# Start and end of an attention and MLP kernel rearranged: two float32 tiles, four DMA transposes, statistics on ScalarE, low halves on GpSimd, and a bank of its own for the last half tile

## The chip, the cores and the metric

The kernel runs on one core of a Trainium2 chip. The metric is the time of one execution on the device in microseconds (us). The engines are TensorE (PE in the profile, with PEld for its weight loads), VectorE (DVE), ScalarE (ACT), GpSimd (POOL) and SyncE (SP), which issues every DMA of this kernel from one queue, in order. Each engine, too, works through its own list in order: an instruction that waits holds up all that stands behind it on that engine.

## The reference

The input x is a sequence of 2048 tokens with 512 channels. It is normalised, and two branches read the result xn; the output is x + s * silu(m).

```python
xn = _layernorm(x)
# A: 32 heads of 16 channels; each token attends to 8 tokens, 2 apart, itself the first
qkv = (xn @ wqkv).reshape(B, S, 3, H, Dh)
logits = q . k at pos - 2*w (w = 0..7), scale Dh**-0.5, masked where pos - 2*w < 0
s = (softmax(logits) applied to v).reshape(B, S, D) @ wo
# B: normalise again, 512 -> 1376 -> 512
y = _layernorm(xn)
h = _gelu(y @ w1 + b1)
m = h @ w2 + b2
return x + s * _silu(m)
```

All arrays are float32.

## The kernel before, in words

**Tiling.** The dilation of 2 splits the tokens into an even and an odd class (c = 0, 1) of 1024 tokens each, and a class into 8 tiles of 128 tokens (i = 0..7). The 32 heads form 4 blocks of 8 heads (hb). A unit u is one class and one block; there are 8 units, class 0 first. For a unit `qkv` (L673) multiplies each of the 8 tiles with a block of 128x384 weights (q, k and v), and ScalarE scales the sums out of PSUM into one of two buffers `U`, alternating. DMAs then shift keys and values by one partition (the halos, L718), and `attention` (L737) works on VectorE with help from GpSimd. `mlp1` and `mlp2` (L948, L983) do the MLP in 4 chunks of 512 tokens and 11 blocks of 128 hidden channels, and are spread between the units as filler for TensorE. `wo_first` and `wo_last` multiply the attention with wo, class 0 in the middle of the program and class 1 at its end.

**Float16 pairs.** TensorE multiplies in float16 with a high and a low half for each operand: three products, hi·hi, lo·hi and hi·lo, so that a tile of `qkv` takes 12 matmuls of 384 columns and a step of the MLP 12 of 512. A high half is a scaled copy (ScalarE, L448, L499, L644); the low half is the source minus the high half (VectorE, L449, L501, L645). The scale is a power of two from the sum of squares of the whole weight, which ScalarE adds up (L394, L477) and TensorE totals over the partitions (L403, L408).

**The start.** `LOADS` (L48) fixes the order of the first loads: `("t", i)` is tile i already transposed, `("q", k)` half of the first or second block of wqkv, `("x", i)` tile i. Behind them come w1 in four pieces, w2, b1 and the rest of w2. Tiles 5, 6 and 7 (`FP`) get their first `qkv` in float32, straight from the transposed input: the mean is taken off (`center`, L557) and `direct` (L575) multiplies, 4 matmuls of 384 columns for a tile, with no transposition and no halves needed. The others go through `ln0` (statistics, L586), `y0` (normalise on the engine that `Y_ENG` names, transpose on TensorE, L641, then the two halves) and 12 matmuls each. Tiles 5 to 7 go through `y0` later for the second unit and the MLP. 24 matmuls without use (L1102, `WAKE`) fill gaps early on.

**Class 1.** `ln1` (L647) normalises the odd tokens: eight loads and statistics on VectorE (L542, L543), factors for all tiles with two powers on GpSimd (L529, L536), then tile by tile a second load, the normalisation and the halves, and a DMA transposition into `yT` (L666). The load of tile i waits until tile i-2 has been transposed.

**What sets the order.** Every operation is entered in a plan with an engine, an assumed duration, what it reads and writes and a priority. `issue` (L212) then orders each engine by assumed times and priorities. A number such as `PW2` or `PEV` moves whole groups of operations on their engines.

**The end.** `wo_last` (L898) first does 9 of 12 matmuls for each of the 8 tiles of class 1, those of the first three blocks, and the last 3 when the last block is there; VectorE multiplies with the gate (L939), VectorE or GpSimd adds x (L867, L869) and SP sends the tile out. The last tile is finished in two halves of 256 columns (L926, L930, L933), both in one PSUM bank.

Of the kernel before, what the change touches and what calls it, by code (L numbers as in the profile page):

```python
# [31 lines left out]
NFB = 7  # L32

W1C = [0, 2048, 4096, 5120, KT * F]
W1P = [(0, 1), (1, 2), (2, 4), (4, 6), (6, 8), (8, 10), (10, 11)]
W1FIRST = 2
# [4 lines left out]
FP = (5, 6, 7)  # L41
XC = FP
BYDMA = ()
TRZ = (0, 3, 0, 3, 0, 1, 2, 3)
PTR = 0.08
# [11 lines left out]
W2LATE = 4  # L57
# [214 lines left out]
PW2, PS2 = 0.9, 0.74  # L272
PWQ1, PW1 = 0.5, 0.75
PEV = 0.15

PTOT = 0.5

WAKE = 24
PS1 = 0.72
# [12 lines left out]
WINDOW = 0.05  # L292
PURG, WURG = 0.14, 0.05
# [6 lines left out]
def tile_mixer(ctx, tc, a_x, a_xt, a_wqkv, a_wo, b_w1, b_b1, b_w2, out):  # L300
# [171 lines left out]
    def scale_q(hb):  # L472
        col = R_s.new()
        for k in range(0, KT, 2):
            def go(k=k):
# [5 lines left out]
                aps=2, holds=stkey[hb])  # L481
# [7 lines left out]
    def prep_q(hb):  # L489
# [3 lines left out]
        for k in range(0, KT, st):  # L493
# [7 lines left out]
            dve(n, lambda src=src, dst=dst: nc.vector.scalar_tensor_tensor(  # L501
                dst[1], src(), qsc[:, hb, 0:1], dst[0], op0=ALU.mult, op1=ALU.subtract),
                r + hk, [("wq", hb, j) for j in range(k, k + st)], holds=stkey[hb], c=0.125,
                prio=PQLO if hb == 0 else None)

# [5 lines left out]
    def factors(n, mv, mk, cdst, ckeys, bias=True, close=None, pp=None, **k):  # L511
# [19 lines left out]
        with pl.fuse():
            dve(n, lambda: nc.vector.tensor_scalar(a0(), V(), EPS, None, op0=ALU.add), mk, [(A, 0)], c=0.15)
            dve(n, lambda: nc.vector.reciprocal(a1(), a0()), [(A, 0)], [(A, 1)], c=0.2)
            dve(n, lambda: nc.vector.tensor_tensor(a1(), a1(), V(), op=ALU.mult), [(A, 1)] + mk, [(A, 1)], c=0.2)
            dve(n, lambda: nc.vector.tensor_scalar(a1(), a1(), EPS, None, op0=ALU.add), [(A, 1)], [(A, 1)], c=0.2)
        pool(0.42 + 0.14 * n, lambda: nc.gpsimd.tensor_tensor(  # L536
            cdst, a1(), halves[:, 8:8 + n], op=ALU.pow), [(A, 1)], ckeys, port=False)
        return rb, p0b
# [18 lines left out]
    def center(i):  # L557
# [11 lines left out]
        pe(1, P, lambda: nc.tensor.matmul(b.t[:, 0:P], mean1, f3()[:, 0], start=True, stop=True), [f], [b], fp32=6, prio=0.04)  # L569
# [42 lines left out]
    def y0(i):  # L612
# [5 lines left out]
        if Y_ENG[i] == "act":  # L618
            with pl.fuse("act"):
# [4 lines left out]
                    [xkey, ("rb", g), ("rm", i)], [xkey, yk], aps=2)  # L624
        else:
            dve(512, lambda: nc.vector.tensor_scalar(x(), x(), mv0[:, q, 0:1], rb0[:, q:q + 1], op0=ALU.subtract,
                                                     op1=ALU.mult), [xkey, ("rb", g), ("mv0", i)], [xkey, yk], f=0.72, c=0.11)
        if i in BYDMA:
# [6 lines left out]
                [y16, (y16, 0)], [("yh", 0, i), ("y", 0, i)], rate=150e3, issue=2.1, tail=1.4)  # L635
# [6 lines left out]
        pe(4, P, tr, [yk, xkey], [b], fp32=2.4, prio=PTR + pl.prio * 1e-3)  # L642
        p3 = lambda: b.t.rearrange("p (k t) -> p k t", k=KT)
        act(512, lambda: nc.scalar.copy(hi, p3()), [b], [("yh", 0, i)], aps=0)  # L644
        dve(512, lambda: nc.vector.tensor_tensor(lo, p3(), hi, op=ALU.subtract), [b, ("yh", 0, i)], [("y", 0, i)], port=False)  # L645

    def ln1():  # L647


        mv1 = sb.tile([P, NI, 2], F32, name="mv1")  # L650
        mk = [("mv1", i) for i in range(NI)]
# [4 lines left out]
        rb = factors(NI, lambda: mv1, mk, cT[:, 1, :], [("c", 1, i) for i in range(NI)])  # L656
        for i in range(NI):
# [4 lines left out]
            y_act(lambda x=x: x.t, rb, i, [], lambda x=x: x.t, x)  # L662
# [8 lines left out]
    IORD, IORD0, IORD1 = [1, 2, 3, 4, 5, 6, 7, 0], [5, 6, 7, 0, 1, 2, 3, 4], [0, 1, 2, 3, 4, 5, 6, 7]  # L671

    def qkv(c, hb, u):  # L673
# [10 lines left out]
                [("c", c, i) for i in g] + ([("rb", gof[i]) for i in g] if g[0] in FP else [("qi", hb)]), [(cs, g)], prio=0.15)  # L684
# [4 lines left out]
        for n, i in enumerate((IORD0, IORD1)[u] if u < 2 else IORD):  # L689
# [14 lines left out]
            for n0, n1 in zip([0] + ends, ends):  # L704
# [3 lines left out]
            act(384, lambda i=i, b=b: nc.scalar.activation(  # L708
                U3[:, i:i + 31:15, :], b.t[:, 0:384].rearrange("p (t e) -> p t e", t=3),
# [356 lines left out]
    for n in range(4):  # L1066
        load_w1(n)
# [231 lines left out]
```

## Time and profile before

| | |
|---|---|
| three executions | 419.18, 419.77 and 420.14 us, median 419.77 |
| the profiled execution | 420.04 us, its span 418.3 us |
| granted TensorE clock | 1.000 |
| TensorE busy | 408.4 us (98%) |
| VectorE busy | 386.3 us (92%) |
| ScalarE busy | 213.6 us (51%) |
| GpSimd busy | 110.7 us (26%) |

The profile has a page for the whole execution and views that can be asked for a stretch of time. In a row of the timeline stand the start and the duration in us, the engine, the line, the operation, what is written from what, the shape and the count; in brackets, the idle time before it and what ended that. A float32 matmul leaves two records. The span is 1.7 us shorter than the execution that it belongs to.

### The profile page before, as it was taken

The numbers are of one execution on the slowest core, as the hardware profiler recorded it, in microseconds if no ns is written. First come the engines' busy times: TensorE is split into PE (matmuls) and PEld (weight loads), VectorE is DVE, ScalarE is ACT, GpSimd is POOL, SyncE is SP. The second block draws the span as 40 slices with busy tenths as digits, with TensorE's granted clock in tenths as the row PEclk, the third lists the DMA queues.
The fourth block names the chain that finished last, engine by engine and source line by source line (L and its number), as shares of the span: only waits on it lengthen the run. The fifth ranks groups of instructions, "written<-read, shape, count | busy, mean of one in ns | idle before, by whom it ended". The sixth has DMA issues, their size and how long they took to land.

```text
span 418.3 us, 5534 instructions
## 1 busy us (share of the span) xinstructions
PE 408.4 (98%) x2082; PEld 207.4 (50%) x2082; DVE 386.3 (92%) x395; ACT 213.6 (51%) x322; POOL 110.7 (26%) x124
## 2 busy tenths in 40 slices
PE   8899999999999999999999999999999999999995
PEld 5466544444654455445544554455445544444442
DVE  5977899999999999899999899999999998999974
ACT  3899993952539335764475336133322285236400
POOL 3310200004340555021523160425042504250022
PEclk9999999999999999999999999999999999999999
DMA  7955360220047203746275007021623465008142
GB/s 270 415 214 147 98 209 2 86 91 0 1 114 187 67 1 84 155 101 98 55 139 202 0 21 193 2 76 29 208 78 102 110 143 163 0 2 235 33 134 100
DMA packets 43130, 45.62 MB, mean 109 GB/s; under 512 B 27576, under 2 KB 28016, under 8 KB 42592
## 3 DMA queue, kind: packets, MB, share of 16 engines
q1 hardware_dynamic: 43104, 45.28, 37.6%
q8 instruction: 16, 0.26, 0.3%
q14 instruction: 10, 0.08, 0.1%
HBM read 24.32 MB, written 7.34 MB: 76 GB/s over the span
## 4 chain that ended last, share of the span: by engine, by line
PE 68%; DVE 15%; issue 7%; ACT 5%; DMA 3%; SPq 1%; POOL 0%; DVEq 0%; ACTq 0%
PE z L992 19%; PE ps L698 19%; PE ps L956 18%; PE ps L876 7%; DVE prod L810 3%; PE z L876 2%; DVE prod L752 2%; DVE w L449 2%; DVE h L978 2%; DMA prod<-in_A_x_dram 2%; PE pl L698 1%; DVE f L664 1%; DVE L L755 1%; DMA U<-U 1%; DVE prod L805 1%
## 5 line engine op out<-in xcount | busy, mean ns | idle before, releaser
L956 PE MATMUL ps<-yT,w 128*128 128x512 f16 (+1 forms) x528 | 120.8, 379 | 0.5 <-DVE h L978 0.5
L698 PE MATMUL ps<-wq,yT 128*128 128x384 f16 x696 | 115.9, 326 | 1.4 <-ACT yT L644 0.8
L992 PE MATMUL z<-w,h 128*128 128x512 f16 x480 | 110.3, 379 | 0.2 <-ACT f L1008 0.2
L698 PEld LDWEIGHTS <-yT 128*128 128x128 f16 x732 | 71.1, 98 | 50.6 <-issue 1.2
L956 PEld LDWEIGHTS <-w 128*128 128x128 f16 (+1 forms) x528 | 52.9, 100 | 61.5 <-issue 0.8
L973 ACT ACTIVATE ps<-ps,b1T,hsc 128x512 f32<-128x512 f32 (+1 forms) x44 | 32.8, 748 | 86.3 <-PE ps L956 86.2
L752 DVE TENSOR_TENSOR prod<-U 128x2048 f32<-128x2048 f32 x32 | 74.3, 2326 | 2.1 <-DMA U<-U 1.0
L992 PEld LDWEIGHTS <-h 128*128 128x128 f16 x480 | 46.7, 98 | 55.7 <-issue 0.5
L755 DVE TENSOR_REDUCE L<-prod 128x128 f32<-128x2048 f32 x32 | 72.9, 2280 | 0.4
L810 DVE TENSOR_TENSOR prod<-pl,U 128x2048 f32<-128x2048 f32 x28 | 63.2, 2281 | 1.8 <-POOL prod L820 1.8
L708 ACT ACTIVATE U<-ps,cs 128x384 f32<-128x384 f32 x58 | 33.6, 581 | 58.1 <-PE ps L698 57.9
L820 POOL TENSOR_TENSOR prod<-prod,prod 128x2048 f32<-128x2048 f32 x7 | 31.7, 4526 | 115.1 <-DVE prod L810 115.1
L830 POOL TENSOR_TENSOR prod<-prod 128x1024 f32<-128x1024 f32 x14 | 32.8, 2345 | 0.0
L978 DVE SCALAR_TENSOR_TENSOR h<-ps,hsc,h 128x512 f16<-128x512 f32 x40 | 29.3, 740 | 2.7 <-ACT h L976 2.6
L876 PE MATMUL ps<-wo,oT 128*128 128x512 f16 x132 | 29.8, 379 | 0.0
L876 PEld LDWEIGHTS <-oT 128*128 128x128 f16 x189 | 18.5, 98 | 22.1
L829 POOL COPY gate<-prod 1x1 f32<-1x1 f32 x21 | 4.4, 211 | 88.4 <-DVE prod L752 88.4
L976 ACT ACTIVATE h<-ps,hsc 128x512 f16<-128x512 f32 x40 | 26.9, 685 | 0.8
L805 DVE TENSOR_TENSOR prod<-prod,prod 128x2048 f32<-128x2048 f32 x9 | 20.5, 2280 | 0.0
L973 ACT ACT_TABLE_LOAD x10 | 12.8, 1283 | 9.2 <-PE ps L956 9.1
L830 POOL TENSOR_TENSOR prod<-prod,prod 128x1024 f32<-128x1024 f32 x7 | 16.4, 2347 | 0.0
L793 ACT ACTIVATE o<-prod,osc 128x1024 f16<-128x1024 f32 (+1 forms) x9 | 9.5, 1053 | 12.2 <-POOL prod L830 6.8
(165 smaller groups left out, 356.4 us busy)
## 6 DMA issues: line engine op xcount, KB each, us to landing
f<-in_A_x_dram SPq DMA_DIRECT2D x31, 256.0 KB, 3.4
U<-U SPq DMA_DIRECT2D x16, 392.0 KB, 4.0
gd<-f SPq DMA_DIRECT2D x12, 256.0 KB, 2.9
prod<-in_A_x_dram SPq DMA_DIRECT2D x8, 256.0 KB, 6.3
oT<-in_B_w_dram SPq DMA_DIRECT2D x2, 1024.0 KB
yT<-in_B_w_dram SPq DMA_DIRECT2D x2, 1024.0 KB, 12.1
f<-gd SPq DMA_DIRECT2D x8, 256.0 KB, 2.9
out_dram<-f SPq DMA_DIRECT2D x8, 256.0 KB
```

The costliest lines, as they stand in the source:

```text
L698: nc.tensor.matmul(b.t[:, 0:384], y[:, s, k, o:o + P], wq[:, hb, t, k], start=(n == 0), stop=(n == 11))
L708: act(384, lambda i=i, b=b: nc.scalar.activation(U3[:, i:i + 31:15, :], b.t[:, 0:384].rearrange("p (t e) -> p t e", t=3), AF.Identity, sca ...
L752: dve(2048, lambda p2=p2, g=g: nc.vector.tensor_tensor(p2(), q, slots(Ut, KH, 2 * g), op=ALU.mult), qk + [("kh", ub, 0), ("kh", ub, 1), (" ...
L755: dve(2048, lambda pr=pr, g=g: nc.vector.tensor_reduce(L3()[:, 2 * g:2 * g + 2], pr.t.rearrange("p (r f d) -> p r f d", r=2, d=DH), AX.X, ...
L810: dve(2048, lambda: nc.vector.tensor_tensor(pr.t.rearrange("p (r f d) -> p r f d", r=2, d=DH), A3()[:, 2 * g:2 * g + 2].rearrange("p r (f ...
L820: pool(4.75, lambda: nc.gpsimd.tensor_tensor(acc.t, acc.t, p1.t, op=ALU.add), [acc, p1], [acc])
L830: nc.gpsimd.tensor_tensor(x.t[:, 0:1024], x.t[:, 0:1024], y(), op=ALU.add)
L876: nc.tensor.matmul(b.t, oT[:, hb, i // 4, s, i % 4], wo[:, t, hb], start=(hb == 0 and n == 0), stop=(hb == last and n == 2))
L956: nc.tensor.matmul(b.t[0:M], w1[:, s, f * 512 + k * M:f * 512 + (k + 1) * M], yT[ch][:, t, k], start=(n == 0), stop=(n == 11))
L973: act(512, lambda: nc.scalar.activation(b.t[0:M], b.t[0:M], AF.Gelu_apprx_tanh, bias=b1T[0:M, f:f + 1], scale=hsc[0:M, 1:2]), [b, ("b1T",) ...
L978: dve(512, lambda: nc.vector.scalar_tensor_tensor(lo()[0:M], b.t[0:M], hsc[0:M, 2:3], hi()[0:M], op0=ALU.mult, op1=ALU.subtract), [b, hk], ...
L992: nc.tensor.matmul(z.t, hl[s][0:K, t * P:(t + 1) * P], w2[0:K, w, f], start=(f == 0 and n == 0), stop=(f == NF - 1 and n == 2))
```

## The change

It alters the start of the program, `ln1` and `wo_last`, and many of the plan's numbers.

- **Float32 tiles.** Only tiles 6 and 7 are multiplied in float32. Tile 7 gets its mean from four matmuls (`MEANBY`), no longer from GpSimd. Tile 5 goes the way of the others for its first `qkv`.
- **DMA transposes.** Tiles 4 to 7 (`BYDMA`) are no longer transposed on TensorE: their halves are made in SBUF, and a DMA transposes them. These DMAs wait until all of w1 has landed, and the loads of w2 wait for them. Tiles 0 to 3 keep the transposition on TensorE.
- **Order of loads.** `LOADS` covers w1, w2 and b1 as well, and tile 2 is loaded ahead of tile 0.
- **Engines.** Tables name the engine of each small step: the normalisation of tiles 0 and 5 and four low halves (two of the first block of wqkv, one of w1, one of w2) go to GpSimd, as two instructions each; the results of 4 tiles of the first unit and 3 of the second leave PSUM on VectorE.
- **Statistics of class 1.** ScalarE takes them: a pass for the sum, a small one for minus the mean, a pass for the squares.
- **The end.** The second half of the last tile gets a bank of its own and does all its 12 matmuls after the first half is done.

```diff
-W1FIRST = 2
+W1FIRST = 3
-FP = (5, 6, 7)
-XC = FP
-BYDMA = ()
-TRZ = (0, 3, 0, 3, 0, 1, 2, 3)
-GROUPS = [(0,), (1,), (2, 3, 4), (5, 6, 7)]
-BATCHES = [(0, 1, 2, 3, 4), (5, 6, 7)]
-LOADS = [("t", 5), ("t", 6), ("q", 0), ("q", 2), ("x", 0), ("x", 1), ("t", 7), ("q", 4), ("q", 6), ("x", 2), ("x", 3),
-         ("x", 4), ("x", 5), ("x", 6), ("x", 7)]
+FP = (6, 7)
+XC = (6, 7)
+BYDMA = (4, 5, 6, 7)
+TRZ = (3, 3, 0, 2, 0, 1, 1, 0)
+GROUPS = ((0,), (1, 2), (3, 4, 5), (6, 7))
+BATCHES = ((0, 1, 2, 3, 4, 5), (6, 7))
+LOADS = (('t', 6), ('q', 0), ('q', 2), ('x', 2), ('x', 0), ('q', 4), ('t', 7), ('x', 5), ('x', 1), ('x', 3), ('x', 4), ('q', 6), ('w', 0), ('w', 2), ('x', 7), ('c', 2), ('s', 1), ('c', 0), ('w', 3), ('x', 6), ('w', 1), ('c', 1), ('b', 0), ('s', 0))
+HI_ENG = ('act', 'act', 'act', 'dve', 'dve', 'dve', 'dve', 'act')
-Y_ENG = {0: "act", 1: "dve", 2: "act", 3: "act", 4: "act", 5: "dve", 6: "dve", 7: "dve"}
-W1ENG = ["dve", "dve", "act", "act", "act", "act", "act"]
+Y_ENG = ('pool', 'act', 'dve', 'dve', 'act', 'pool', 'dve', 'act')
+W1ENG = ('act', 'dve', 'act', 'act', 'act', 'act', 'act')
-W2LATE = 4
+W2LO = ('dve', 'dve', 'dve', 'dve', 'dve', 'pool', 'dve')
+EV0 = ('act', 'dve', 'dve', 'act', 'act', 'act', 'dve', 'dve')
+EV1 = ('dve', 'dve', 'act', 'act', 'act', 'act', 'dve', 'act')
+QLO0 = ('pool', 'dve', 'dve', 'pool')
+W1LO = ('dve', 'dve', 'pool', 'dve', 'dve', 'dve', 'dve')
+MEANBY = ('dve', 'pe', 'pool', 'pool')
+W2LATE = 6
...
+    def low_pool(n, lo, get, s, hi, **k):
+        def fn():
+            nc.gpsimd.tensor_scalar(get(), get(), s, 1.0, op0=ALU.mult, op1=ALU.mult)
+            nc.gpsimd.tensor_tensor(lo, get(), hi, op=ALU.subtract)
+        pool(0.45 + n * 3.9e-3, fn, **k)
...
+        elif Y_ENG[i] == "pool":
+            pool(1.25, lambda: nc.gpsimd.tensor_scalar(x(), x(), mv0[:, q, 0:1], rb0[:, q:q + 1], op0=ALU.subtract,
+                                                       op1=ALU.mult), [xkey, ("rb", g), ("mv0", i)], [xkey, yk])
...
             dma(P * 2048, lambda: nc.sync.dma_start_transpose(
                 dst.rearrange("p a k t -> p (a k) t")[:, :, o:o + P], y16.t.bitcast(F16)),
-                [y16, (y16, 0)], [("yh", 0, i), ("y", 0, i)], rate=150e3, issue=2.1, tail=1.4)
+                [y16, (y16, 0)] + [k for n in range(4) for k in s1k[n]], [("yh", 0, i), ("y", 0, i)], rate=140e3, issue=1.6, tail=1.2)
...
-            stats(lambda: mv1, i, mk[i], lambda x=x: x.t, [x])
+            act(512, lambda x=x, i=i: nc.scalar.activation(x.t, x.t, AF.Identity, accum_out=mv1[:, 0, i:i + 1]),
+                [x], [x, ("ms", i)], aps=2)
+            act(1, lambda i=i: nc.scalar.activation(mv1[:, 1, i:i + 1], mv1[:, 0, i:i + 1], AF.Identity, scale=-1.0 / D),
+                [("ms", i)], [("mn", i)])
+            act(512, lambda x=x, i=i: nc.scalar.activation(x.t, x.t, AF.Square, bias=mv1[:, 1, i:i + 1],
+                                                           accum_out=mv1[:, 2, i:i + 1]), [x, ("mn", i)], [x, ("mv1", i)], aps=3)
...
+            if (EV0[i] if u == 0 else EV1[i] if u == 1 else "act") == "dve":
+                dve(384, lambda i=i, b=b: nc.vector.tensor_scalar(
+                    U3[:, i:i + 31:15, :], b.t[:, 0:384].rearrange("p (t e) -> p t e", t=3),
+                    cs.t[:, cp(i):cp(i) + 1], None, op0=ALU.mult), c=0.12, port=False, **ev)
...
+        parts = [(i, slice(0, D)) for i in range(NI - 1)] + [(NI - 1, slice(0, LASTP)), (NI - 1, slice(LASTP, D))]
+        for n, (i, cols) in enumerate(parts[:NI]):
+            b = banks[n] = rings[n].new()
+            pe(9, w, mm(b, i, early, cols, True, False), rw + [("A", 7)] * (rings[n] is R_pl), [b], prio=end + 2 * n)
...
+                b = R_ps.new()
+                pe(12, w, mm(b, i, range(NHB), cols, True, True), rw + [("oT", hb, i // 4) for hb in late], [b],
+                   prio=end + 2 * n + 1)
```

Three places show what the plan makes of it. In its rows a word like `yT_83` is a buffer with its number, and the brackets hold the semaphores that an instruction waits for (`DMAHW..` those of DMAs; each of the eight is used again by the eighth DMA after). First, SP's queue from the last loads of the input on, before:

```order
L1039 DMA prod_95<-in_A_x_dram 128x512 [waits DMAHW6_49]
L1064 DMA oT<-in_B_w_dram 128x2048 [waits DMAHW7_49]
L1064 DMA oT<-in_B_w_dram 128x2048 [waits DMAHW0_49]
L1064 DMA o_105<-in_B_w_dram 128x1024 [waits DMAHW1_49]
L1064 DMA h_106<-in_B_w_dram 128x384 [waits DMAHW2_49]
L1069 DMA yT_84<-in_B_w_dram 128x2048 [waits DMAHW3_49]
L1070 DMA yT_85<-in_B_w_dram 128x2048 [waits DMAHW4_49]
L718 DMA U_86<-U_86 112x896 [waits DMAHW5_49,Activation_49]
```

and after:

```order
L1099 DMA prod_95<-in_A_x_dram 128x512 [waits DMAHW0_49]
L1126 DMA oT<-in_B_w_dram 128x2048 [waits DMAHW1_49]
L675 DMA_TRANSPOSE yT_83<-f_97 128x8x128 [waits DMAHW2_49,DVE_49,Activation_49]
L675 DMA_TRANSPOSE yT_83<-f_98 128x8x128 [waits DMAHW3_49,DVE_49]
L1132 DMA b1T<-in_B_b_dram 128x11 [waits DMAHW4_49]
L916 DMA f_101<-in_A_x_dram 128x512 [waits DMAHW5_49]
L675 DMA_TRANSPOSE yT_83<-f_99 128x8x128 [waits DMAHW6_49,DVE_49]
L675 DMA_TRANSPOSE yT_83<-f_100 128x8x128 [waits DMAHW7_49,DVE_49]
L916 DMA f_102<-in_A_x_dram 128x512 [waits DMAHW0_49]
L1134 DMA f_96<-in_B_w_dram 128x512 [waits DMAHW1_49,PE_49]
L1129 DMA yT_85<-in_B_w_dram 128x2048 [waits DMAHW2_49]
L771 DMA U_86<-U_86 112x896 [waits DMAHW3_49,DVE_49,Activation_49]
```

The four transposes stand between the last piece of w1 (`oT`) and the loads of w2 (`f_96`, `yT_85`), and most of w2 now comes behind the first unit's halos (`U_86`). Second, GpSimd at the factors of class 1 (`lw`, `cT`), before, behind the big add of the second unit (L820):

```order
L830 TENSOR_TENSOR prod_95<-prod_95,prod_93 128x1024 [waits Pool_49]
L820 TENSOR_TENSOR prod_94<-prod_94,prod_95 128x2048 [waits DVE_49,Pool_49]
L529 TENSOR_TENSOR lw_132<-lw_131,halves 128x8 [waits DVE_49]
L536 TENSOR_TENSOR cT<-lw_133,halves 128x8 [waits DVE_49]
L829 COPY gate<-prod_95 1x1 [waits DVE_49]
L830 TENSOR_TENSOR prod_94<-prod_94 128x1024 [waits Pool_49]
```

and after:

```order
L883 TENSOR_TENSOR prod_93<-prod_93 128x1024
L819 MEMSET L_104 1x56
L563 TENSOR_TENSOR lw_133<-lw_131,halves 128x8
L570 TENSOR_TENSOR cT<-lw_132,halves 128x8 [waits DVE_49]
L882 COPY gate<-prod_94 1x1 [waits DVE_49]
L883 TENSOR_TENSOR prod_95<-prod_95,prod_93 128x1024 [waits Pool_49]
L873 TENSOR_TENSOR prod_94<-prod_94,prod_95 128x2048 [waits DVE_49,PE_49,Pool_49]
```

The two powers now stand ahead of the second unit's big add (L873), one unit earlier. Third, VectorE's last rows, before:

```order
L930 SCALAR_TENSOR_TENSOR U_86<-z_146,osc,U_86 128x256 [waits PE_49]
L930 SCALAR_TENSOR_TENSOR U_86<-z_146,osc,U_86 128x256
L933 TENSOR_TENSOR U_86<-U_86 128x256 [waits DMAHW0_49,DVE_49]
L933 TENSOR_TENSOR U_86<-U_86 128x256 [waits DVE_49]
```

and after:

```order
L993 SCALAR_TENSOR_TENSOR U_86<-z_146,osc,U_86 128x256 [waits PE_49]
L1000 TENSOR_TENSOR U_86<-U_86 128x256 [waits DMAHW3_49,DVE_49]
L993 SCALAR_TENSOR_TENSOR U_86<-ps_139,osc,U_86 128x256 [waits PE_49]
L1000 TENSOR_TENSOR U_86<-U_86 128x256 [waits DVE_49]
```

One wait for TensorE covered both halves; now each half has its own.

More of the change, by code (lines that the diff above doesn't have):

```diff
@@ L500, in prep_q @@
                 dst[0], src(), AF.Identity, scale=qsc[:, hb, 0:1]), r, hk, holds=stkey[hb])
[L501 to L504, printed above, removed]
+            lo = dict(r=r + hk, w=[("wq", hb, j) for j in range(k, k + st)], holds=stkey[hb], prio=PQLO if hb == 0 else None)
@@ L899, in wo_last @@
         rings = [R_ps, R_ps, R_ps, R_pl] + R_z
[L900 to L905 removed]
+        end = PR_M * 10
+        early, late = range(NHB - 1), [NHB - 1]
+        rw = [("oT", hb, h) for hb in early for h in range(2)] + [("wo", k) for k in (0, 2)]
@@ L1094, in tile_mixer @@
             second(g)
-    with prio(0.55):
-        for i in FP:
+    for i in FP:
+        with prio(PY[i]):
             y0(i)
+    for kind, i in LOADS:
+        if kind in "sc":
+            load(kind, i, [("y", 0, j) for j in BYDMA])
     zero_halo(0)
@@ L1177, in tile_mixer @@
     pl.prio = PW2
-    for k in W2P:
+    for m, k in enumerate(W2P):
         n, K = (2, P) if k < 8 else (1, P if k < NF - 1 else FL + 1)
```

250 lines of the change are left out of this document (142 added, 108 removed).

## Prediction

> **What bounds the kernel now.** I read the page first, then a table of stretches, then timelines where TensorE stands still. The page's first part names the engine:
>
> ```profile
> PE 408.4 (98%) x2082; PEld 207.4 (50%) x2082; DVE 386.3 (92%) x395; ACT 213.6 (51%) x322; POOL 110.7 (26%) x124
> ```
>
> TensorE is busy for all but 9.9 us, so a gain needs less work on it or fewer of these idle microseconds. The table of stretches shows where they are (start and end, length, then busy time and count of each engine, clock, DMA share, GB/s):
>
> ```profile
> 0.00:7.00 7.00, 5.23 (x24) 3.60 (x24) 3.72 (x7) 1.46 (x2) 3.38 (x12) 1.00 0.67 214
> 7.00:17.00 10.00, 9.86 (x39) 5.66 (x40) 7.78 (x26) 7.47 (x16) 2.88 (x5) 1.00 1.04 403
> 17.00:26.00 9.00, 7.02 (x45) 3.96 (x44) 8.31 (x29) 8.66 (x16) 3.01 (x4) 1.00 1.00 407
> 26.00:48.00 22.00, 22.00 (x144) 13.90 (x143) 15.43 (x27) 21.75 (x40) 2.35 (x1) 1.00 0.37 112
> 48.00:65.00 17.00, 16.48 (x79) 7.48 (x78) 16.90 (x23) 16.80 (x27) 0.66 (x5) 1.00 0.49 146
> 65.00:124.00 59.00, 59.00 (x302) 29.45 (x301) 58.28 (x68) 27.99 (x40) 12.61 (x15) 1.00 0.15 49
> 124.00:206.00 82.00, 81.40 (x421) 41.24 (x419) 79.27 (x68) 48.13 (x77) 26.49 (x20) 1.00 0.42 95
> 206.00:300.00 94.00, 93.76 (x488) 47.62 (x486) 90.00 (x67) 39.63 (x53) 28.78 (x35) 1.00 0.33 89
> 300.00:386.00 86.00, 86.00 (x424) 41.81 (x423) 82.93 (x63) 35.94 (x47) 25.41 (x26) 1.00 0.39 108
> 386.00:419.00 33.00, 27.67 (x132) 12.63 (x129) 23.64 (x25) 5.81 (x8) 5.08 (x4) 1.00 0.30 96
> ```
>
> From 26 us on TensorE almost never waits until the tail. What can be won: the time before the second unit's matmuls run without a break, 0.5 us at 48 to 65, 0.6 at 124 to 206, and the tail. TensorE's own timeline gives the prices of the start:
>
> ```profile
> 15.06 2.10 PE L578 MATMUL z<-prod,U 128*128 128x384 f32 x6
> ...
> 17.05 1.56 PE L698 MATMUL ps<-wq,yT 128*128 128x384 f16 x8
> ...
> 27.38 1.04 PE L641 MATMUL z<-ident,prod 128*128 128x128 f32 x8
> ...
> 30.64 2.11 PE L698 MATMUL pl<-wq,yT 128*128 128x384 f16 x12
> 32.59 2.76 PE L698 MATMUL ps<-wq,yT 128*128 128x384 f16 x16
> ...
> 48.26 7.93 PE L956 MATMUL ps<-yT,w 128*128 128x512 f16 x36
> ...
> 64.79 2.75 PE L956 MATMUL ps<-yT,w 128*128 128x512 f16 x12 [0.46 <-DVE h L978]
> ```
>
> Three float32 matmuls (six records) take 2.10, so a float32 tile of four 2.7. A tile transposed on TensorE takes 1.04/2 = 0.5. A float16 tile takes 32.59 - 30.64 = 1.95. The first float16 tile starts at 17.05, the MLP at 48.26.
>
> **The change, step 1: TensorE up to the MLP.** Removed: one float32 tile (2.7) and four transpositions (2.1). Added: one float16 tile (1.95) and two more matmuls for a mean (about 0.4). That is 2.4 us less work, but it counts only as far as the data come in time. From 17.05 to 48.26 are 31.2 us, filled with 5 + 8 float16 tiles (25.4), 6 transpositions (3.2) and about 0.6 of small totals: 29.2, and 2.0 of waiting. After the change the same part holds 6 + 8 tiles (27.3), 3 transpositions (1.6) and the totals: 29.5. So the shift comes from when the first float16 tile starts and from the new waits.
>
> The loads' pace is read from two tiles that VectorE waits for:
>
> ```profile
> 8.47 0.70 DVE L542 BATCH_NORM_STATS2 bn<-prod 128x6 f32<-128x512 f32 x1 [1.51 <-DMA prod<-in_A_x_dram]
> ...
> 11.52 0.69 DVE L542 BATCH_NORM_STATS2 bn<-prod 128x6 f32<-128x512 f32 x1 [0.41 <-DMA prod<-in_A_x_dram]
> ...
> 13.73 0.54 DVE L626 TENSOR_SCALAR prod<-prod,mv,rb 128x512 f32<-128x512 f32 x1
> 14.19 0.61 DVE L501 SCALAR_TENSOR_TENSOR wq<-prod,qsc,wq 128x384 f16<-128x384 f32 x1
> ...
> 15.54 0.66 DVE L645 TENSOR_TENSOR yT<-z,yT 128x512 f16<-128x512 f32 x1
> ```
>
> Tile 0 is there at 8.47 with 1,536 KB loaded, tile 2 at 11.52 with 2,688 KB: 2.65 us for 1,000 KB. In the new order tile 0 again ends at 1,536 KB, the transposed tile 7 comes at 10.2, tiles 1, 3 and 4 at 11.5, 12.2 and 12.9, and the last of w1 (6,848 KB) at 22.5. For GpSimd I use these rows:
>
> ```profile
> 16.35 0.86 POOL L596 TENSOR_TENSOR rb<-pb,halves 128x3 f32<-128x3 f32 x1 [4.12 <-DVE pb L594]
> 20.11 1.17 POOL L609 TENSOR_TENSOR cT<-aa,halves 128x5 f32<-128x5 f32 x1 [2.90 <-DVE pb L592]
> ...
> 411.94 1.26 POOL L869 TENSOR_TENSOR U<-U,f 128x512 f32<-128x512 f32 x1 [1.97 <-DVE U L939]
> ```
>
> Its normalisation (a tensor_scalar over 512) has no row; between nothing and twice the two-input 1.26 I take 1.26. Tile 7: mean to 11.1, subtracted behind tile 5's statistics by 12.8; TensorE transposes tile 0 at 12.5 to 13.1 and then does tile 7 in float32 to 15.8. Tile 0's halves are ready by 13.6 and 16.1. So the first float16 tile starts at 15.85, 1.2 earlier. Its eight matmuls end at 17.3. Then tiles 3, 2 and 1 must be normalised: VectorE, behind three statistics (to 15.4), has the low half of tile 0 (0.66), a weight's low half (0.61), about 1.2 of small operations and tile 3 (0.54), so 18.3: 1.0 us of waiting. About 0.7 more I give to evictions that now wait on VectorE's list. 15.85 + 29.5 + 1.7 = 47.05, against 48.26: **-1.2**. From none of these waits and float32 work at once (44.9) to 2 us more of them (49) it is -3.4 to +0.8.
>
> **Step 2: the DMA transposes.** They cost TensorE nothing if they land in time. Eight of the same form are in the trace:
>
> ```profile
> L666 SPq DMA_TRANSPOSE yT<-f x8: 1232/1238/2664, 162.2 to 204.7; - x8
> ...
> DMA to landing us min/median/max: 3.1/4.7/5.2
> ```
>
> Tile 4's is held by w1 (22.5) and its low half (about 23.4) and lands near 28.2; TensorE's list comes to it at 30.4. Tile 7's is issued at about 29.9 and lands at 34.6 to 35.1; it is wanted at 36.0. Slack of 2.2 and 1.0: no cost. Behind them on SP wait b1, two tiles of class 1, the rest of w2 and the halos of the first unit. For w2 the cover is the new order of the MLP: six first halves (6 x 12 matmuls at 7.93/36 = 0.22, so 15.6 us) stand ahead of the first use of w2.
>
> **Step 3: the MLP's start.** The 0.5 us of waiting at 48 to 65 goes, since the first h is used six steps later: **-0.5**, with a chance of up to 2 us of new waits where w2's low halves come late.
>
> **Step 4: class 1.** TensorE waits for the last transposition there:
>
> ```profile
> 201.91 3.08 DMA yT<-f
> 205.03 2.12 PE ps L698 x12
> ```
>
> The row of the statistics shows why it is late, and GpSimd's second power, when the tiles could begin:
>
> ```profile
> L542 DVE BATCH_NORM_STATS2 bn<-f x8: 636/683/687, 96.7 to 143.0; 128x6 f32<-128x512 f32 x8
> ...
> 150.90 3.62 POOL L536 TENSOR_TENSOR cT<-lw,halves 128x8 f32<-128x8 f32 x1 [4.30 <-DVE lw L535]
> ...
> 44.99 0.62 ACT L1164 ACTIVATE w<-f 128x512 bf16<-128x512 f32 x1
> 45.51 0.19 ACT L1164 ACTIVATION_READ_ACCUMULATOR w<-f 128x1 f32 x1
> ```
>
> VectorE loses 8 x (0.68 + 0.18) = 6.9 us, ScalarE gains 8 x (2 x 0.8 + 0.25) = 15 us, in a stretch where it is busy 28.0 of 59.0. The powers move up one unit, so the eight tiles begin some 35 us earlier and the wait of 0.6 goes: **-0.6**.
>
> **Step 5: the tail.** In the timeline VectorE starts both halves only when TensorE is done:
>
> ```profile
> 412.85 0.82 PE L926 MATMUL z<-wo,oT 128*128 128x256 f16 x6
> ...
> 413.71 0.88 DVE L930 SCALAR_TENSOR_TENSOR U<-z,osc,U 128x256 f32<-128x256 f32 x2 [1.85 <-PE z L926]
> 414.50 0.75 DVE L933 TENSOR_TENSOR U<-U 128x256 f32<-128x256 f32 x2
> 414.94 0.81 SPq L935 DMA_DIRECT2D out_dram<-U  x2
> ```
>
> The last add ends 1.57 after TensorE. With a bank for each half, the first is finished during the 12 matmuls of the second (1.3 us), and one multiplication and one add are left, 0.9: **-0.7** (0 to -0.9). The work on TensorE is the same, 24 x 256 columns.
>
> **A price the trace puts on GpSimd.** A two-input operation of VectorE (2.33 on average) took 3.67 when it started beside a GpSimd add:
>
> ```profile
> 154.61 2.35 POOL L830 TENSOR_TENSOR prod<-prod 128x1024 f32<-128x1024 f32 x1
> 155.44 3.67 DVE L752 TENSOR_TENSOR prod<-U 128x2048 f32<-128x2048 f32 x1
> ```
>
> In my sum nothing of this stands. If it holds for the powers, lows and normalisations at 16 to 22 us, the low half of the weight there waits 0.6 and the two normalisations on VectorE up to 1.3: 1.9 us. The Trainium skill states it as a rule (SBUF — State Buffer, section on SBUF's two separate sides): GpSimd and a VectorE operation with two SBUF inputs, or in a two-port mode, lock the shared ports for a whole instruction. This row agrees. By the rule the sum would be 1.9 higher; I keep the lower one, because most of VectorE's operations there read PSUM or have one input.
>
> **The sum.** 420.04 of the profiled execution - 1.2 - 0.5 - 0.6 - 0.7 = 417.0. That execution lies 0.3 above the median of 419.77, so against the median I say 416.8.
>
> **Rivals.**
> - *GpSimd holds up VectorE.* For it the row of 3.67, against it the kind of operations: 416.8 + 1.9 = 418.7, still faster.
> - *Transposes land late: slower.* The first unit's tiles 4 and 5 and all of the second half of class 0 hang on them, and TensorE's list is in order. For it: the trace's eight are spread over 162.2 to 204.7, 6 us apart on the mean; here they are 1.2 to 2.9 apart, with loads beside them. If they ran strictly one after another at 8 us each, tile 5 would land at 23.5 + 16 = 39.5 where it is wanted at 34: +5.5, so 422.3. It decides above 7.4 us each: tile 5 is then 4.3 late, which uses up the 3.0 gained and the 0.8 that can be told from no change. Against it: 5.2 is the longest seen.
> - *The gain is lost in the middle: no change.* If the class 1 tiles stay as late as 205, TensorE arrives earlier and waits: only the tail's 0.7 is left, 419.1. The earlier powers speak against it.
> - *The start runs without waits.* 44.9 instead of 47.05: 414.7.
>
> **How the numbers follow.** Likeliest case 0.57; GpSimd 0.12; no waits 0.12; middle 0.06; slower 0.13. A measurement here can tell about 0.2%, 0.84 us, from no change: 418.9 to 420.6 is the same. Faster 0.80 (likeliest, GpSimd and no waits, all but a little), same 0.07, slower 0.13. The range takes in the no-wait start, with 0.3 for a tail at its lower bound, and the lost middle with 0.3 more; it leaves out the slower case and little else: 414.4 to 419.4.
>
> **What would show it.** Right: the first float16 tile near 16, the MLP's first matmul at 46 to 48, no break between 48 and 65, no wait for `yT` in the middle, one multiplication and one add behind TensorE's last matmul. Wrong: TensorE waiting for the DMA transposes at 30 to 36 us, w2's total holding up the MLP's fifth step, or VectorE's rows at 16 to 22 us drawn out.

## The result and the profile after

The changed kernel takes 414.88 us (median of four executions, 414.58 to 415.18); the kernel before, on the same chip, 419.95 (four, 419.18 to 421.18). The ratio is 0.988, 95% interval 0.985 to 0.990. The forecast was 416.8, range 414.4 to 419.4: the direction is right, the gain of 5.1 us is larger than the 3.0 reckoned.

The profiled execution took 415.18 us, its span 413.4 instead of 418.3. The first part of its page:

```profile
PE 405.9 (98%) x2083; PEld 206.6 (50%) x2083; DVE 379.5 (92%) x379; ACT 222.1 (54%) x353; POOL 120.3 (29%) x131
```

TensorE does 2.5 us less work (408.4 to 405.9) and stands still for 7.5 us instead of 9.9. Together that is the 4.9 us of the span, so half is work and half is waiting. The table of stretches of the changed kernel, cut as before, shows where the waiting went (a stretch's length less TensorE's busy time; the span ends at 413.4):

```profile
0.00:7.00 7.00, 5.73 (x24) 3.77 (x25) 2.14 (x5) 2.38 (x4) 3.39 (x12) 1.00 0.70 221
7.00:17.00 10.00, 8.23 (x42) 4.94 (x41) 9.00 (x29) 5.33 (x12) 5.25 (x6) 1.00 1.04 407
17.00:26.00 9.00, 8.32 (x53) 5.06 (x52) 8.63 (x25) 8.90 (x16) 6.25 (x6) 1.00 0.55 187
26.00:48.00 22.00, 21.92 (x135) 12.80 (x133) 18.09 (x33) 21.00 (x41) 6.44 (x4) 1.00 0.79 231
48.00:65.00 17.00, 17.00 (x81) 7.68 (x80) 15.66 (x18) 14.82 (x22) 0.00 (x0) 1.00 0.41 119
...
124.00:206.00 82.00, 81.96 (x428) 42.01 (x427) 78.90 (x60) 48.41 (x75) 25.28 (x26) 1.00 0.37 86
206.00:300.00 94.00, 94.00 (x485) 47.26 (x483) 91.13 (x68) 39.38 (x52) 25.66 (x27) 1.00 0.35 108
```

Up to 48 us TensorE waits as long as before, 3.8 instead of 3.9: 2.0 at 17 to 26 became 0.7, but 0.1 at 7 to 17 became 1.8. From 48 to 300 us, 1.36 of waiting became 0.04. The waits that are left, from the view of what TensorE waited for (us in total, times, longest):

```profile
PE z L683 <- POOL prod L665: 1.6, 1, 1.6
PE z L1169 <- DVE fours L365: 1.2, 1, 1.2
PE z L683 <- DVE prod L668: 0.4, 1, 0.4
PE ps L746 <- DVE U L759: 0.2, 1, 0.2
```

None is for a DMA transpose. TensorE's timeline in the changed kernel, with the steps that the forecast had dated:

```profile
12.86 0.66 PE L683 MATMUL z<-ident,prod 128*128 128x128 f32 x4 [1.65 <-POOL prod L665]
...
15.96 0.81 PE L746 MATMUL ps<-wq,yT 128*128 128x384 f16 x4
...
17.84 1.85 PE L683 MATMUL z<-ident,prod 128*128 128x128 f32 x12 [0.40 <-DVE prod L668]
...
24.44 5.36 PE L746 MATMUL ps<-wq,yT 128*128 128x384 f16 x32 [0.19 <-DVE U L759]
...
46.22 10.52 PE L1016 MATMUL ps<-yT,w 128*128 128x512 f16 x48
```

The first float16 tile starts at 15.96 (reckoned 15.85), the MLP at 46.22 (reckoned 47.05; before 48.26). The end of TensorE and the tail:

```profile
408.29 1.47 PE L961 MATMUL ps<-wo,oT 128*128 128x256 f16 x12
...
409.80 0.48 DVE L993 SCALAR_TENSOR_TENSOR U<-ps,osc,U 128x256 f32<-128x256 f32 x1 [0.29 <-PE ps L961]
410.32 0.42 DVE L1000 TENSOR_TENSOR U<-U 128x256 f32<-128x256 f32 x1
```

TensorE's last matmul ends at 409.76, 3.91 earlier than before (413.67). So the MLP starts 2.04 earlier, another 1.87 is gained from there to TensorE's end, and 0.99 behind it.

### The profile page after: what moved, and what is told of

Its sections match the earlier page's. It is cut to its first block, busy times and chain, and to the rows that moved or that the text cites. A ratio compares the mean times of both kernels' runs of the same rounds, so it can differ in the third digit from the quotient of the medians.

```text
span 413.4 us, 5554 instructions
## 1 busy us (share of the span) xinstructions
PE 405.9 (98%) x2083; PEld 206.6 (50%) x2083; DVE 379.5 (92%) x379; ACT 222.1 (54%) x353; POOL 120.3 (29%) x131
## 4 chain that ended last, share of the span: by engine, by line
PE 92%; ACT 3%; issue 1%; DVE 1%; POOL 1%; ACTq 0%
PE z L1052 28%; PE ps L1016 28%; PE ps L746 25%; PE ps L929 5%; PE ps L961 2%; PE z L961 2%; PE pl L746 1%; ACT w L421 1%; PE pl L961 1%; ACT f L673 1%; ACT yT L687 0%; ACT wq L536 0%; POOL wq L471 0%; POOL rb L635 0%; ACT prod L661 0%
## 5 line engine op out<-in xcount | busy, mean ns | idle before, releaser
L746 PEld LDWEIGHTS <-yT 128*128 128x128 f16 x744 | 72.5, 98 | 49.2 <-issue 1.0
L805 DVE TENSOR_TENSOR prod<-U 128x2048 f32<-128x2048 f32 x32 | 73.2, 2286 | 2.2 <-POOL prod L883 0.7
L763 ACT ACTIVATE U<-ps,cs 128x384 f32<-128x384 f32 x54 | 31.2, 580 | 65.2 <-PE ps L746 65.2
L873 POOL TENSOR_TENSOR prod<-prod,prod 128x2048 f32<-128x2048 f32 x7 | 31.7, 4531 | 113.8 <-DVE prod L863 99.6
L882 POOL COPY gate<-prod 1x1 f32<-1x1 f32 x21 | 5.5, 264 | 91.0 <-DVE prod L805 82.2
L929 PE MATMUL ps<-wo,oT 128*128 128x512 f16 x96 | 21.7, 379 | 0.0
L961 PEld LDWEIGHTS <-oT 128*128 128x128 f16 x108 | 10.6, 98 | 10.4
L929 PEld LDWEIGHTS <-oT 128*128 128x128 f16 x96 | 9.4, 98 | 11.2
```

Of the source, the lines that this page charges most:

```text
L746: nc.tensor.matmul(b.t[:, 0:384], y[:, s, k, o:o + P], wq[:, hb, t, k], start=(n == 0), stop=(n == 11))
L763: act(384, lambda i=i, b=b: nc.scalar.activation(U3[:, i:i + 31:15, :], b.t[:, 0:384].rearrange("p (t e) -> p t e", t=3), AF.Identity, sca ...
L805: dve(2048, lambda p2=p2, g=g: nc.vector.tensor_tensor(p2(), q, slots(Ut, KH, 2 * g), op=ALU.mult), qk + [("kh", ub, 0), ("kh", ub, 1), (" ...
L873: pool(4.75, lambda: nc.gpsimd.tensor_tensor(acc.t, acc.t, p1.t, op=ALU.add), [acc, p1], [acc])
L929: nc.tensor.matmul(b.t, oT[:, hb, i // 4, s, i % 4], wo[:, t, hb], start=(hb == 0 and n == 0), stop=(hb == last and n == 2))
L961: nc.tensor.matmul(b.t[:, cols], oT[:, hb, i // 4, s, i % 4], wo[:, t, hb, cols], start=(start and hb == 0 and n == 0), stop=(stop and hb ...
```

## Experiments

All were timed in rounds with the kernel before. Three groups of four ran on the same chip each. The second group (three float32 tiles to old start) has no run of the changed kernel in it, so there I compare with the medians 414.88 to 415.10 from other chips. A label names the variant of the changed kernel, unless it says "old start".

**The yardstick.**

> The changed kernel once more, on the same chip and in the same rounds as the three that follow, so that each can be compared with it. Both theories: 414.9 +- 0.5, 5 below the kernel before.

Measured: 415.10 (414.77 to 415.27), ratio 0.988 [0.986, 0.990].

**The old tail.** `wo_last` is that of the kernel before, which also gives the add of the last whole tile to GpSimd (408.12 to 409.39, done before TensorE ends).

```diff
-                b = R_ps.new()
-                pe(12, w, mm(b, i, range(NHB), cols, True, True), ...)
+                    pe(3, 256, mm, [("oT", NHB - 1, i // 4)] + ([b] if h == 0 else []), [(b, "h", h)], ...)
```

> The changed kernel with the end of the kernel before (both halves of the last tile in one bank). Theory (the trace's readings add up, and the tail is worth what its rows show): 0.6 to 1.0 more than the changed kernel, near 415.7, with the stretch from TensorE's last matmul to the end of the span back from 3.6 to 4.6. Rival (the last store's landing sets the end and varies by itself): no difference that can be told.

Measured: 415.63 (415.34 to 416.97), 0.53 more. Its timeline has the old form again:

```profile
409.03 0.82 PE L979 MATMUL z<-wo,oT 128*128 128x256 f16 x6
409.88 0.88 DVE L983 SCALAR_TENSOR_TENSOR U<-z,osc,U 128x256 f32<-128x256 f32 x2 [1.85 <-PE z L979]
410.68 0.75 DVE L986 TENSOR_TENSOR U<-U 128x256 f32<-128x256 f32 x2
```

From TensorE's end (409.85) to the last add (411.43) are 1.58, against 0.98 with the new tail: 0.60 is the bank's worth. From the last add to the end of the span it is 2.77 here, 2.66 in the changed kernel and 3.05 before. So the other 0.39 of the 0.99 lies in the landing of the last store; 2.77 with the old tail shows that most of it (0.28) isn't the tail's form.

**The old statistics of class 1.**

```diff
-            act(512, lambda x=x, i=i: nc.scalar.activation(x.t, x.t, AF.Identity, accum_out=mv1[:, 0, i:i + 1]), ...)
+            stats(lambda: mv1, i, mk[i], lambda x=x: x.t, [x])
```

> The changed kernel with the statistics of class 1 on VectorE and the two powers as before. Theory (the tiles of class 1 came too late for TensorE): 0.6 to 1.0 more, with TensorE waiting for yT near 200 again, and perhaps more since TensorE arrives 3 us earlier: up to 3.5 if the whole of the start's gain is waited away there, 418.4. Rival (the wait was chance of the plan, and the gain came from elsewhere): less than 0.3, and no wait for yT.

Measured: 416.67 (416.03 to 417.14), 1.57 more. Two of the waits of TensorE that the changed kernel hasn't (us in total, times, longest), and then rows of its timeline:

```profile
PE ps L749 <- DVE h L1041: 0.9, 1, 0.9
...
PE z L1055 <- ACT f L1071: 0.2, 1, 0.2
```

```profile
194.16 7.96 PE L749 MATMUL ps<-wq,yT 128*128 128x384 f16 x48 [0.93 <-DVE h L1041]
...
202.51 1.82 PEld L749 LDWEIGHTS <-yT 128*128 128x128 f16 x12 [0.23 <-DMA yT<-f]
```

The place is the one foretold (class 1's first `qkv`, 189 to 208), and the size lies between the two ends given. The wait has another form, though: only 0.23 is a wait for `yT`; with the 0.2 ahead of L1055 the three make 1.4 of the 1.57. The 0.93 ends with VectorE's low half of an h; that `qkv` waits for this is put down by the semaphore, and I read it as a PSUM bank that VectorE, late with the low halves of class 1 in its list, hadn't let go. That reading wasn't tested apart.

**All transpositions on TensorE.**

```diff
-BYDMA = (4, 5, 6, 7)
+BYDMA = ()
```

> The changed kernel with tiles 4 to 7 transposed on TensorE, so that no DMA transposes class 0 and w2's loads wait for none. Theory (start bound by TensorE's work, the DMA transposes hidden): 4 x 0.52 = 2.1 us more work for TensorE, so 1.5 to 2.5 more, MLP's first matmul near 48.3, not 46.2. Rival (start bound by when data are ready, TensorE has gaps that the transpositions fill): less than 0.7 more.

Measured: 417.35 (417.02 to 418.60), 2.25 more. The theory holds: 4 x 0.52 = 2.1 us of TensorE's work is paid nearly in full, so at this place TensorE's list is full. The profiled execution (418.03) is above the median for a reason of its own. Its windows and the float32 tile in it:

```profile
11.00:13.00 2.00, 0.54 (x3) 0.54 (x4) 1.97 (x5) 0.49 (x2) 1.41 (x1) 0.89 1.08 428
13.00:15.00 2.00, 2.00 (x6) 1.34 (x5) 1.85 (x8) 1.42 (x3) 0.02 (x1) 0.50 0.98 403
15.00:17.00 2.00, 2.00 (x6) 1.05 (x5) 1.96 (x6) 0.00 (x0) 1.92 (x3) 0.76 1.02 393
```

```profile
12.46 1.07 PE L683 MATMUL z<-ident,prod 128*128 128x128 f32 x4 [1.65 <-POOL prod L665]
13.33 4.06 PE L617 MATMUL z<-prod,U 128*128 128x384 f32 x8
```

After 1.65 of idle time the granted clock is 0.50 (the column before the last two) and the tile takes 4.06; in the other kernels it takes 2.75. So its MLP start (48.92) holds 1.3 of clock. The median execution does not rest on that: the three with a mean granted clock of 1.000 took 417.02 to 417.41.

**Three float32 tiles.**

```diff
-FP = (6, 7)
-GROUPS = ((0,), (1, 2), (3, 4, 5), (6, 7))
-LOADS = (('t', 6), ...
+FP = (5, 6, 7)
+GROUPS = ((0,), (1, 2), (3, 4), (5, 6, 7))
+LOADS = (('t', 5), ('t', 6), ...
 # and TRZ, BATCHES, MEANBY and IORD0 to match
```

> The changed kernel with tile 5 again multiplied in float32 for its first qkv (three float32 tiles, its mean on VectorE, its transposed load first in the queue). Theory (TensorE's work decides): a float32 tile of 2.7 in place of a float16 tile of 1.95 is 0.75 more work, so 0.5 to 1.5 more than the changed kernel, MLP's first matmul at 46.7 to 47.7. Rival (TensorE waits for data until 18 us, 1.65 + 0.40 of it behind the normalisations, and a third float32 tile fills that): 0 to 1 less, without the wait of 1.65.

Measured: 429.56 (427.91 to 430.93), 14.5 more: both theories missed. The wait of 1.65 is gone, but the plan put the total of w1's squares (L435), the first use of w2 (1.0 and 1.7) and a step of the MLP at 141 us (2.5) ahead of their data:

```profile
PE z L1052 <- ACT f L1068: 2.9, 2, 2.5
PE z L435 <- ACT w L421: 2.6, 1, 2.6
...
PE z L1052 <- DVE w L486: 1.7, 1, 1.7
```

All its waits are 13.8, against 3.4 in the changed kernel. So this run prices a wrong order, not a float32 tile. What the third tile alone is worth stays open.

**Nothing of the low halves or normalisations on GpSimd.**

```diff
-Y_ENG = ('pool', 'act', 'dve', 'dve', 'act', 'pool', 'dve', 'act')
-QLO0 = ('pool', 'dve', 'dve', 'pool')
+Y_ENG = ('act', 'act', 'dve', 'dve', 'act', 'act', 'dve', 'act')
+QLO0 = ('dve', 'dve', 'dve', 'dve')
 # W1LO and W2LO all 'dve' too
```

> The changed kernel with GpSimd's four low halves back on VectorE and its two normalisations on ScalarE. Theory (VectorE has the work in hand at 12 to 18 us, GpSimd relieves it): four low halves of 0.6 to 1.3 more on VectorE, 0.5 to 2 more. Rival (GpSimd's instructions hold VectorE up, one small operation took 0.88 in place of 0.14 beside them, and GpSimd's normalisation of 2.08 makes TensorE wait for 1.65): no slower, or up to 1 faster, with the small operation back at 0.15.

Measured: 416.71 (416.50 to 417.77), 1.7 more than the medians of the changed kernel (414.88 to 415.10). GpSimd's help is worth having, as the theory said. The rival's sign came too (two L633 in 0.23 instead of one in 0.88), but without its gain.

**Tile 0's normalisation on ScalarE.** One word of the same table.

```diff
-Y_ENG = ('pool', 'act', 'dve', 'dve', 'act', 'pool', 'dve', 'act')
+Y_ENG = ('act', 'act', 'dve', 'dve', 'act', 'pool', 'dve', 'act')
```

> The changed kernel with the normalisation of tile 0 alone on ScalarE (about 0.8 and a small one of 0.3) in place of GpSimd (2.08). Theory (the wait only moves: after the first float16 tile TensorE needs tiles 3, 2 and 1, which VectorE has at 17.8): within 0.3 of the changed kernel, the 1.65 ahead of tile 0's transposition shorter by 0.5 to 1 and the 0.40 at 17.84 longer by as much. Rival (GpSimd's 2.08 is on the path): 0.5 to 1 less.

Measured: 414.04 (413.92 to 414.67), ratio 0.987 [0.986, 0.989]. TensorE's timeline:

```profile
11.51 0.63 PE L683 MATMUL z<-ident,prod 128*128 128x128 f32 x4 [1.02 <-issue]
...
16.50 1.11 PE L683 MATMUL z<-ident,prod 128*128 128x128 f32 x8 [0.44 <-DVE prod L668]
...
45.09 10.52 PE L1016 MATMUL ps<-yT,w 128*128 128x512 f16 x48
```

My theory falls. The first wait shortens by 0.6, and the second does not grow (0.44 against 0.40), since VectorE's list came forward as well. It was not tile 0's low half that brought it forward: VectorE's first low half (L543) starts 0.69 earlier in this execution (9.39 instead of 10.08), tile 0's low half behind it 0.68 earlier (13.75 instead of 14.43), while tile 3's normalisation starts 1.34 earlier (15.91 instead of 17.25). The other 0.66 lies in L633, which took 0.88 in the changed kernel and 0.15 here; what held it up stands under "The rivals". The 0.69 is a difference between executions: in two other profiles of the changed kernel L543 starts at 9.72 and 10.10. So of the 1.13 at the MLP's start about 0.4 is the move's.

**The new class 1 and tail, the old start.** The kernel before, with `ln1` and `wo_last` of the changed one.

> The kernel before with the new statistics of class 1 (ScalarE) and the new tail, its start as it was. Theory (the parts add up): the start is worth 2.0 up to the MLP and 0.9 from there to 104 us, so this kernel lies 2.5 to 3.5 above the changed kernel and 1.5 to 2.5 below the kernel before, near 417.8. Rival (the gains overlap: TensorE that arrives 3 us earlier would wait in the middle without the earlier class 1, and class 1 alone is worth nothing at the old pace): 0.7 to 1.2 below the kernel before, near 418.8.

Measured: 418.25 (417.42 to 418.64), 1.37 below the kernel before in the same rounds (419.62), between the two numbers given, so neither expectation is met. The start is then worth some 3.2 (418.25 less 415.0). The wait that Step 3 had at 48 to 65 is still in it, at 64.09:

```profile
64.09 2.75 PE L963 MATMUL ps<-yT,w 128*128 128x512 f16 x12 [0.46 <-DVE h L985]
```

**The changed kernel in the third group.**

> The changed kernel again, as the yardstick for the three that follow on the same chip: 414.9 +- 0.5.

Measured: 414.98 (414.71 to 415.17), ratio 0.990 [0.988, 0.991].

**All results of the first two units leave PSUM on ScalarE.**

```diff
-EV0 = ('act', 'dve', 'dve', 'act', 'act', 'act', 'dve', 'dve')
-EV1 = ('dve', 'dve', 'act', 'act', 'act', 'act', 'dve', 'act')
+EV0 = ('act',) * 8
+EV1 = ('act',) * 8
```

> The changed kernel with all results of the first two units leaving PSUM on ScalarE. Theory (the evictions on VectorE, to which the prediction gave 0.7 of waiting, cost nearly nothing, since only 0.19 of waiting is seen, and ScalarE has no room): 7 evictions of 0.6 each go to an engine that is busy for 20.99 of 22.00 us at 26 to 48, so 0.5 to 2 more. Rival (they hold TensorE up): 0.2 to 0.7 less.

Measured: 423.36 (422.71 to 423.94), 8.4 more: the right sign and four times the size. TensorE's waits and the table of stretches show how:

```profile
PE z L1052 <- ACT w L482: 3.9, 1, 3.9
PE z L1052 <- DVE w L486: 2.0, 1, 2.0
```

```profile
64.00:68.00 4.00, 0.38 (x1) 0.10 (x1) 3.90 (x9) 3.76 (x6) 0.17 (x2) 0.88 0.00 0
68.00:72.00 4.00, 3.78 (x9) 1.28 (x9) 4.00 (x5) 2.79 (x4) 1.72 (x1) 0.50 0.56 165
72.00:76.00 4.00, 4.00 (x16) 1.67 (x15) 3.37 (x3) 2.92 (x10) 1.70 (x2) 0.77 0.91 315
```

The last pass for w2's sum of squares and w2's first high half, on ScalarE, in the changed kernel:

```profile
52.97 1.90 ACT L421 ACTIVATE w<-yT 128x2048 bf16<-128x2048 f32 x1
...
57.77 3.23 ACT L482 ACTIVATE w<-yT,zsc 128x1024 f16<-128x1024 f32 x3 [0.24 <-DVE zsc L454]
```

and in this variant:

```profile
57.53 1.90 ACT L421 ACTIVATE w<-yT 128x2048 bf16<-128x2048 f32 x1
...
64.69 4.26 ACT L482 ACTIVATE w<-yT,zsc 128x1024 f16<-128x1024 f32 x4 [0.24 <-DVE zsc L454]
```

Seven evictions of 0.57 are 4.0 on an engine that is busy for 21.0 of 22.0 us, and w2's sum is 4.6 later, its halves 6.9 (the total behind the sum now also stands behind two products on VectorE, whose L439 starts at 63.93 instead of 57.03). TensorE waits 5.85, and in the 8 us after that its clock is 0.50 and 0.77, another 2.9 (4 x 0.50 + 4 x 0.23). The MLP's start is not later (46.29 against 46.24), so the evictions cost nothing up to there; their price comes behind it.

**Tiles 0 and 5 both on ScalarE.**

```diff
-Y_ENG = ('pool', 'act', 'dve', 'dve', 'act', 'pool', 'dve', 'act')
+Y_ENG = ('act', 'act', 'dve', 'dve', 'act', 'act', 'dve', 'act')
```

> The changed kernel with the normalisations of tiles 0 and 5 both on ScalarE, GpSimd keeping its four low halves. Theory (GpSimd's normalisation of tile 0 was on the path, that of tile 5 was not): as with tile 0 alone, 0.8 to 1.1 less than the changed kernel, near 414.0; the difference to the kernel that has GpSimd's low halves on VectorE as well is then the price of these, 2.5 or more. Rival (ScalarE is full, so tile 5 there costs what tile 0 gains): within 0.3 of the changed kernel.

Measured: 418.05 (416.95 to 418.77), 3.1 more; both expectations missed, the rival's reason is the nearer one:

```profile
25.25 3.41 PE L746 MATMUL ps<-wq,yT 128*128 128x384 f16 x20 [1.84 <-ACT U L763]
```

ScalarE has no time left at 17 to 26 (8.90 of 9.00 in the changed kernel's table); I read the late eviction as the price of tile 5's 1.1 there, which was not tested apart. This wait and one of 0.72 for w2's low half, less some 0.4 for tile 0, are the 2.1 by which the profiled execution (417.26) is longer; of the slower executions there is no trace. This kernel is also slower than the one with GpSimd's low halves on VectorE as well (416.71, on another chip), so a price of the low halves can't be read off as a difference: the parts don't add up.

**Tile 0 alone, beside the yardstick.**

> The normalisation of tile 0 alone on ScalarE, once more, in the same rounds as the changed kernel. Theory (the 2.08 of GpSimd was on the path): 0.8 to 1.1 less than the changed kernel in the same rounds. Rival (the earlier difference was one between chips): less than 0.4 apart.

Measured: 414.60 (414.27 to 414.78), 0.38 below the changed kernel in the same rounds. In the two profiles of these rounds the MLP starts at 45.54 and 46.24 and the spans are 412.7 and 413.4. That is less than the 0.8 to 1.1 expected and within the rival's 0.4. L543 starts at 9.85 and 10.10, so 0.25 of the 0.70 lies ahead of the move, and some 0.45 is its own, as in the first run. The gain is seen in both traces; it is at the edge of what the times can tell.

## Why the prediction was right, and where its sizes were off

**Step 1, up to the MLP: reckoned -1.2, measured -2.04.** The start of the first float16 tile was right to 0.11, and so was the work behind it: 46.22 - 15.96 less 0.59 of waiting is 29.67, reckoned 29.5. The term that was mis-sized is the new waits, 1.0 and 0.7 reckoned, 0.40 and 0.19 measured: 0.11 + 0.17 - 1.11 = -0.83 is the whole difference between 47.05 and 46.22. The 48.26 it starts from is one execution, though: in the run with the old start the same matmuls begin the first float16 tile at 16.34 and the MLP at 47.57, 0.7 earlier, because the first weights are there sooner (`direct` starts at 6.05 instead of 6.93, where TensorE had waited 0.59 for them). Against that execution the shift is 1.35, close to the 1.2 reckoned. The 1.0 of waiting came from a guess at VectorE's list. Its rows:

```profile
10.73 2.08 POOL L665 TENSOR_SCALAR prod<-prod,mv,rb 128x512 f32<-128x512 f32 x1
...
11.43 0.67 DVE L610 TENSOR_TENSOR U<-U,ps 128x512 f32<-128x512 f32 x1
...
15.00 0.94 POOL L471 TENSOR_TENSOR wq<-prod,wq 128x384 f16<-128x384 f32 x1
15.01 0.16 DVE L631 TENSOR_SCALAR pb<-mv 128x3 f32<-128x3 f32 x1
15.07 0.88 DVE L633 TENSOR_SCALAR pb<-mv 128x3 f32<-128x3 f32 x1
...
15.90 1.55 POOL L635 TENSOR_TENSOR rb<-pb,halves 128x3 f32<-128x3 f32 x2
15.94 0.17 DVE L633 TENSOR_SCALAR pb<-mv 128x2 f32<-128x2 f32 x1
16.02 0.60 DVE L543 SCALAR_TENSOR_TENSOR wq<-prod,qsc,wq 128x384 f16<-128x384 f32 x1
...
17.25 1.00 DVE L668 TENSOR_SCALAR prod<-prod,mv,rb 128x512 f32<-128x512 f32 x2
```

Tile 3 is normalised half a microsecond earlier than reckoned (18.3). That the start at 15.96 came out right is partly luck: GpSimd's normalisation took 2.08, not 1.26, so tile 0 held TensorE until 12.86 with tile 7 ready since 12.10; but it began at 10.73, half a microsecond before the 11.24 that the forecast's 12.5 less 1.26 allows, and that took most of the error away. Tile 0's move to ScalarE brings some 0.4 at the MLP's start.

**Step 2, the DMA transposes: no cost, as reckoned.** The row of all four:

```profile
L675 SPq DMA_TRANSPOSE yT<-f x4: 1240/1248/1351, 22.8 to 29.3; - x4
...
DMA to landing us min/median/max: 3.5/3.5/3.5
```

They land between 26.3 and 32.8; the forecast had 28.2 to 35.1, with some 5 each. With them on TensorE the kernel is 2.25 slower. The cover for w2 held with half a microsecond to spare: w2's first low half ends at 61.27 (59.99 and 1.28) and TensorE comes to it at 61.79. The forecast named that cover without saying how thin it is; the evictions on ScalarE show what it costs when it is gone.

**Step 3, the MLP's start: the wait of 0.5 went.** With the old start it is still there.

**Step 4, class 1: the wait of 0.6 went, but the step is worth more.** Undone alone it costs 1.57, and I read that, without a test apart, as TensorE coming 3 us sooner while VectorE's statistics and late low halves stand in the way of other work.

From the MLP's start to TensorE's end -1.87 was measured and -1.1 reckoned (Steps 3 and 4). Waiting at 48 to 300 us accounts for -1.32 (0.24 of it at 206 to 300, which the forecast had left out); the remaining 0.55 is work of TensorE by its busy time. One matmul without use that stood there before (56.03, 0.27) is half of it; the matmuls of `qkv`, of the MLP and of wo work through the same columns in both kernels, so the rest stays open.

**Step 5, the tail: reckoned -0.7, measured -0.99.** VectorE's part is -0.60, and -0.53 by the times of the old tail; 0.39 more is the store's landing.

The five steps were seen where they were forecast; their sizes were off. The measured 414.88 lies only 0.5 above the lower end of the range, and that end stood for a start without waits, which did not come: the 1.9 between -3.0 and -4.9 is 0.8 of step 1, 0.8 behind the MLP's start and 0.3 of the tail.

**The rivals.** Late transposes and a gain lost in the middle did not come. GpSimd did hold VectorE up, in one place: L633 started beside GpSimd's L471 at 15.07, ended with it at 15.95 and took 0.88, where the same instruction took 0.15 with tile 0 on ScalarE. By the Trainium skill (SBUF — State Buffer, section on SBUF's two separate sides) the later of the two is blocked until the first is done, if VectorE's operation has two inputs in SBUF or runs in a two-port mode. These two rows agree in time; L633 has one input, and no run shows its mode. Beside GpSimd's other work the rows don't agree: L543, with two inputs in SBUF, started within the powers of L635 and took 0.60 (0.61 before, at 14.19), and L674, also with two, started at 22.04 within GpSimd's normalisation of tile 5 (20.54 to 22.62) and took 0.68 (0.69 at 24.55, with GpSimd idle). The forecast priced the powers and normalisations with the subtractions, and left the whole out because most of VectorE's operations there have one input or read PSUM; the one that was held up has one input, so its reason was wrong though leaving the 1.9 out was right. The price is 0.7 on VectorE and at most 0.40 on TensorE. The rival with no waits at all (414.7) is closest in time, though 2.2 us of waiting at 11 to 25 are left.

## What to carry to other kernels

On an engine that is 98% busy, count work and waiting apart: here half of the gain was 2.5 us less work on TensorE, some 2.1 of it the four transpositions that went to DMA, and guessed waits ate more of it in the forecast than in the run. Before an engine takes a task over, look at its busy share in that very stretch: ScalarE, busy for 8.90 of 9.00 and 21.0 of 22.0 us, made two small moves cost 3.1 and 8.4 us, while at 7 to 17 us, where it was busy for 5.33 of 10.00, it took tile 0's normalisation at a gain of 0.4. And a wait on the bounding engine is dearer than its length if the clock falls behind it: 5.85 us of waiting cost another 2.9.

## What the runs showed of the hardware that I had not expected

- GpSimd's tensor_scalar over 128x512 takes 2.08 us when both scalars come from memory, and 0.69 (L470, 128x512) with one of them a constant (the first also subtracts, so the constant alone wasn't tested); 1,024 elements with a constant take 1.33. The two-input subtraction that writes float16 takes 2.14 for 1,024.
- The DMA transposes of 128x1024 16-bit elements land 3.5 us after the issue, each of four, with loads around them; before, the same form took 3.1 to 5.2.
- The clock of TensorE fell to 0.50 after 5.85 us of waiting (the evictions on ScalarE), and in one execution after 1.65, while other executions with a wait of 1.65 at the same place kept 1.00. The Trainium skill (TensorE: Matmul & The Clock Gate, Part 1 on the clock gate) says that the clock halves after an idle window of about 3.4 us, a window that runs freely. The first case agrees; in the second the wait is half as long, so the length of the wait alone does not decide.
